# Gated linear attention feeding a cosine-gated layer: x's round trip through memory put ahead of the powers' row in SyncE's queue, and one VectorE pair swapped

## The chip, the core and the metric

The kernel runs on one core of one Trainium2 chip. The metric is the device time of one execution in microseconds (us); lower is better. The core's engines run side by side and wait for each other through semaphores: TensorE (PE, its weight loads shown apart as PEld), VectorE (DVE), ScalarE (ACT), GpSimd (POOL) and SyncE (SP). SP computes nothing here. It issues DMA transfers, one after another in a fixed order, and an issue that has to wait holds up all issues behind it.

## What is computed

The reference, cut to what matters:

```python
# q, k, v, a_re, a_im: (4, 8, 768, 48)
mag = sqrt(a_re**2 + a_im**2); scale = minimum(mag, 0.999) / (mag + 1e-6)
a_re_n, a_im_n = a_re * scale, a_im * scale
for t in range(S):                     # S_re, S_im: 48 x 48 per batch and head
    new_re = ar * S_re - ai * S_im
    new_im = ar * S_im + ai * S_re
    S_re, S_im = new_re + outer(k[t], v[t]), new_im
    y[t] = q[t] @ S_re
x = y.transpose(0, 2, 1, 3).reshape(3072, 384)
h = x @ w_in                           # 384 x 2048
out = (h * cos(h)) @ w_out             # 2048 x 384
```

The first part is a linear recurrence with a complex decay for each step and channel; the second is a two-layer network with the gate h cos h.

## The kernel before

The 768 steps of a batch are cut into chunks of 128, and two chunks make a group: 24 chunks, groups 0 to 11. Inside a chunk the recurrence is done by matmuls: the decays become running sums of logs and angles, keys and queries are scaled and turned by them (tiles ks and qs), keys meet queries in the scores (sc), masked scores (atm) times values plus queries times the running state give y, and the state is moved on to the next chunk with the decay over the whole chunk. That decay is the last row of the powers' tile P. It lies along one partition and is wanted along 96, so it goes out to memory and comes back: `row_out` (L843) writes tile `row`, `row_back` (L848) reads it twice into `end`. `p_end` (L858) then scales `end` on VectorE, after keys and queries were turned.

In the same way y, which is made transposed (tile yT, copied out of PSUM by ScalarE in `f_out`), goes to memory and back to become xT, the layout that the first layer's matmuls read: `f_x` (L1063) issues two writes (x<-yT), `f_xt` (L1072) one read (xT<-x). Matmuls of the first layer are called hp, those of the second op and sum (seven half-size products in place of eight, from group 2 on).

The instructions for groups 0 and 1, and for part of group 2, are written out by hand. From there on a loop (L1721) makes one round for each n from 2 to 11. I call it round n. In round n the kernel works on the scores, state and outputs of group n (`chunks`, L1410), on the logs, powers, keys and queries of group n+1 (`logs`, `prods`, `phases`, `keys`), and on the layers of groups n-1 and n. `weave` (L1363) sets the order: every list of steps gets an interval between 0 and 1, its steps are spread evenly over it, and all are sorted by place. The list `chunks(n)` has the interval 0 to 0.36 and 10 steps (9 in rounds 10 and 11, which load nothing): for each of two chunks two halves of scores, the state and the output; then x and xT (`f_x` and `f_xt`); then the load of keys, queries and values of group n+2. The powers (`prods`) stand from 0.2701 to 0.2735, the first hp matmuls at 0.56. A scheduler then settles the order of instructions on each engine from this order and from what each must wait for; `behind(a, b)` forces a after b on one engine.

Before the change `row_out` and `row_back` were issued at the end of `even_steps` (L822), right after P is done, so at about 0.273; x and xT stood at 0.306. All of these, and the loads of re, im, k, q and v, and the moves that turn keys and queries (tr to memory, then kT and qT back), stand in SyncE's one queue. The load of k can be issued only when VectorE has read the old keys (instruction pair<-k, in `p_apply`, L865), the row only when P is done (lg<-pair,lg; P lives in tile lg), xT only when both writes of x have landed.

In `log_steps` (L736), from group 2 on (PEG = 2), logs are split into a high half (hi, on ScalarE) and a low half (lo, on VectorE), and the product mag*sq, which is the first step of a refined reciprocal, is forced behind lo. The lines L680, L691 and L711 are helpers' lines at which the profile books nearly all ordered instructions of VectorE and ScalarE, TensorE, and ScalarE's table functions.

Of the kernel before, what the change touches and what calls it, by code (L numbers as in the profile page):

```python
# [487 lines left out]
def fast_path(ctx, tc, q, k, v, a_re, a_im, moe_w_in, moe_w_out, out, least, odd, wide,  # L488
# [7 lines left out]
    nc = tc.nc  # L496
    B, H, S, D = q.shape
    DM, DF = moe_w_in.shape
    C = 128
    NCH = S // C  # L500
    G = 2
    N = B * NCH
    NG = N // G
# [30 lines left out]
    late = {}  # L534
    tail = {}

    def chain(ins, engine="scalar"):

        if engine in tail:
            behind(ins, tail[engine])  # L540
        tail[engine] = ins

    def behind(ins, other):
        tc.add_manual_dep(ins.ins, other.ins.name, mybir.DependencyInfo(
            mybir.DependencyClass.NoSync, mybir.DependencyReason.DATA))
# [14 lines left out]
    X = [dict() for _ in range(NG)]  # L560
# [4 lines left out]
    PEG, PER = 2, 1  # L565
# [143 lines left out]
    def special(func, **kw):  # L709
        preload(tables[func])  # L710
        chain(nc.scalar.activation(func=func, **kw))  # L711
# [4 lines left out]
    def temp(tag, bufs=1):  # L716
        return gt.tile([C, G * DM], F32, tag=tag, name=tag, bufs=bufs)
# [5 lines left out]
    def cut(t, i, n):  # L723
        return (flat(t) if len(t.shape) == 4 else t)[:, ds(i * DM, n * DM)]

    def upper_half(g, x, scale):


        for name, tag in ("hi", "rs"), ("lo", "lo"):
            X[g][name] = gt.tile([C, G * DM], F32R, tag=tag, name=name)  # L730
        hi, lo = X[g]["hi"], X[g]["lo"]
        chain(nc.scalar.activation(out=hi, in_=x, func=AF.Copy, scale=scale))
        return lambda: vector.scalar_tensor_tensor(
            out=lo, in0=x, scalar=scale, in1=hi.bitcast(F32), op0=ALU.mult, op1=ALU.subtract)

    def log_steps(g, i, n):  # L736


        x = X[g]
        re, im = cut(x["re"], i, n), cut(x["im"], i, n)  # L740
        if i == 0:
            if g == 0:
                x["sin"] = temp("tan", 2)
            for name in "lg", "tan", "rs":
                x[name] = temp(name, 2 if name == "tan" else 1)
            both = gt.tile([C, 2, G * DM], F32, tag="pair", name="pair")
            x["Q"], x["mag"] = both[:, 0], both[:, 1]
        m2, sq, rs, mag = (cut(x[name], i, n) for name in ("lg", "tan", "rs", "mag"))
        for out_, in_ in (m2, re), (sq, im):
            if g == 0 and i > 0:  # L750
                if in_ is im:
                    yield
                vector.tensor_tensor(out=out_, in0=in_, in1=in_, op=ALU.mult)
            else:
                chain(nc.scalar.activation(out=out_, in_=in_, func=AF.Square))
        vector.tensor_tensor(out=m2, in0=m2, in1=sq, op=ALU.add)
        yield
        special(out=m2, in_=m2, func=AF.Ln, bias=tiny_b)
        special(out=mag, in_=m2, func=AF.Exp, scale=0.5)
        if g == 1:  # L760
            yield
        special(out=rs, in_=m2, func=AF.Exp, scale=-0.5)
        yield
        vector.scalar_tensor_tensor(out=mag, in0=re, scalar=0.0, in1=mag,
                                    op0=ALU.max, op1=ALU.add)
        vector.tensor_scalar(out=m2, in0=m2, scalar1=0.5, scalar2=math.log(CAP),
                             op0=ALU.mult, op1=ALU.min)
        yield
        special(out=rs, in_=rs, func=AF.Ln, scale=EPS, bias=one_b)
        special(out=sq, in_=mag, func=AF.Ln)  # L770
        special(out=sq, in_=sq, func=AF.Exp, scale=-1.0)
        yield
        vector.tensor_tensor(out=m2, in0=m2, in1=rs, op=ALU.subtract)
        yield

        lower = upper_half(g, m2, 1.0) if g >= PEG else None
        if lower:
            X[g]["low"] = lower()
        product = vector.tensor_tensor(out=mag, in0=mag, in1=sq, op=ALU.mult)
        if lower:  # L780
            behind(product, X[g]["low"])
        yield
        vector.scalar_tensor_tensor(out=sq, in0=mag, scalar=2.0, in1=sq,
                                    op0=ALU.subtract, op1=ALU.mult)
        yield
        vector.scalar_tensor_tensor(out=sq, in0=sq, scalar=-1.0, in1=im,
                                    op0=ALU.mult, op1=ALU.mult)
        yield
        junk = stage["pool"].tile([C, DM], BF16, tag="below", name="below", bufs=1) if n == 1 else re
        checked = scalar.activation(out=junk, in_=re, func=AF.Relu, scale=-1.0,  # L790
                                    accum_out=odd[:, ds(next(odds), 1)])
        if g > PEG:
            behind(checked, tail["scalar"])

    def g_log(g, i, n):
        for _ in X[g].pop("steps", None) or log_steps(g, i, n):
            pass
# [24 lines left out]
    def even_steps(g, i, n):  # L822


        x = X[g]
        u = cut(x["mag"], i, n)
        P, Q = cut(x["P"], i, n), cut(x["Q"], i, n)
        ins = [vector.scalar_tensor_tensor(out=u, in0=Q, scalar=HUGE, in1=P,
                                           op0=ALU.min, op1=ALU.mult)]
        yield  # L830
        for t in P, Q:
            ins.append(vector.scalar_tensor_tensor(out=t, in0=u, scalar=3.0, in1=t,
                                                   op0=ALU.subtract, op1=ALU.mult))
            yield

        for one_, what in zip(ins, ("carried", "split")):
            if what in x and g > PEG:
                behind(one_, x[what])
        if g > 0:
            row_out(g, i, n, nc.sync)  # L840
            row_back(g, i, n, nc.sync)

    def row_out(g, i, n, queue):  # L843
        P = cut(X[g]["P"], i, n)
        queue.dma_start(out=X[g]["row"][ds(i * DM, n * DM)],
                        in_=P[C - 1:C].rearrange("o x -> (o x)"))

    def row_back(g, i, n, queue):  # L848
        row = X[g]["row"][ds(i * DM, n * DM)]
        end = X[g]["end"][:, ds(i * H, n * H)]  # L850
        for a in range(2):
            queue.dma_start(out=end[ds(a * D, D)], in_=row.rearrange("(x d) -> d x", d=D))
# [122 lines left out]
    def f_scores(n, hh):  # L975
        y, (g, i) = Y[n], divmod(n, G)
        if i == 0 and hh == 0:
            X[g]["atm"] = ft.tile([C, G, H, C], F32, tag="atm", name="atm", bufs=1)
        y["atm"] = X[g]["atm"][:, i]
        ps = pa.tile([C, HH, C], F32, tag="a", name="sc")  # L980
        for h in range(HH):
            head = hh * HH + h
            matmul(ps[:, h], lhsT=X[n // G]["kT"][:, n % G * H + head],
                   rhs=queries(n, head), start=True, stop=True)
        y["masked"] = vector.tensor_tensor(
            out=y["atm"][:, ts(hh, HH)], in0=ps, in1=causal.unsqueeze(1).to_broadcast([C, HH, C]), op=ALU.mult)
        if "whole" in X[n // G - 1]:
            behind(y["masked"], X[n // G - 1]["whole"])
# [68 lines left out]
    def f_state(n):  # L1057
        if n % NCH < NCH - 1:
            state_sums(n)
            for _ in state_next(n):  # L1060
                pass

    def f_x(g, i=0, n=G):  # L1063

        if i == 0:
            X[g]["moved"] = rows_d.tile([HH, 2, D, G, C], F32, tag="x", name="x")
        for side in range(2):
            late["x"] = nc.sync.dma_start(
                out=X[g]["moved"][:, side, :, ds(i, n)].rearrange("p d g t -> d p g t"),
                in_=X[g]["yT"][ds(side * 64, D), :, ds(i, n)])  # L1070

    def f_xt(g, i=0, n=G):  # L1072

        if i == 0:
            X[g]["xT"] = msb.tile([C, ND, G, C], F32, tag="xT", name="xT")
        moved = X[g]["moved"].rearrange("p s d g t -> (p s d) g t").rearrange("(c r) g t -> r c g t", r=C)
        put = nc.sync.dma_start(out=X[g]["xT"][:, :, ds(i, n)], in_=moved[:, :, ds(i, n)])
        behind(put, late["x"])
        late["x"] = put
# [330 lines left out]
    def chunks(g):  # L1410
        for n in range(g * G, g * G + G):
            for hh in range(2):
                yield lambda n=n, hh=hh: f_scores(n, hh)
            yield lambda n=n: f_state(n)
            yield lambda n=n: f_out(n)
        yield lambda: (f_x(g), f_xt(g))
        if g + 2 < NG:
            yield lambda: load(g + 2, ("k", "q", "v"))

# [423 lines left out]
```

## Time and profile before

| what | value |
|---|---|
| median of 3 runs (lowest to highest) | 659.08 us (659.04 to 659.52) |
| profiled execution, its own time | 662.06 us |
| span of the core in the profiled execution | 660.3 us |
| PE busy | 632.5 us (96%) |
| PEld busy | 573.7 us (87%) |
| DVE busy | 522.4 us (79%) |
| ACT busy | 446.5 us (68%) |
| POOL busy | 30.8 us (5%) |
| SyncE's DMA queue (q1) | 225320 packets, 68.51 MB, 44.9% of 16 engines |
| mean granted TensorE clock | 0.992 of full speed |

TensorE is busy nearly all the time, so what can be won without taking work away lies in its few gaps and in stretches at a lower clock. The profile gives for each group of instructions the idle time of the engine just before them and what ended it. Where several semaphores were waited for, it names the one that came last by its own records. A transfer's issue (SPq rows) is short; its landing comes later and shows in the rows of those that wait, and in the chain of waits.

### The profile page before, as it was taken

The numbers are of one execution on the slowest core, as the hardware profiler recorded it, in microseconds if no ns is written. First come the engines' busy times: TensorE is split into PE (matmuls) and PEld (weight loads), VectorE is DVE, ScalarE is ACT, GpSimd is POOL, SyncE is SP. The second block draws the span as 40 slices with busy tenths as digits, with TensorE's granted clock in tenths as the row PEclk, the third lists the DMA queues.
The fourth block names the chain that finished last, engine by engine and source line by source line (L and its number), as shares of the span: only waits on it lengthen the run. The fifth ranks groups of instructions, "written<-read, shape, count | busy, mean of one in ns | idle before, by whom it ended". The sixth has DMA issues, their size and how long they took to land.

```text
span 660.3 us, 11335 instructions
## 1 busy us (share of the span) xinstructions
PE 632.5 (96%) x4279; PEld 573.7 (87%) x4279; DVE 522.4 (79%) x846; ACT 446.5 (68%) x803; POOL 30.8 (5%) x53
## 2 busy tenths in 40 slices
PE   8999989997999999999999999999999999999996
PEld 5888867675899899899899899899899899999996
DVE  6999979769588799879778868979868969965261
ACT  7898677274597498589489489579579479552340
POOL 4010200000000000000000000000000000000000
PEclk9999989998999999999999999999999999999998
DMA  9977744716716925935935945945855853451001
GB/s 241 243 187 192 229 154 98 179 42 143 210 49 141 282 58 121 253 97 127 252 80 136 252 85 137 244 93 144 229 107 144 229 106 110 129 124 50 24 1 32
DMA packets 232924, 94.95 MB, mean 144 GB/s; under 512 B 208701, under 2 KB 221246, under 8 KB 232858
## 3 DMA queue, kind: packets, MB, share of 16 engines
q1 hardware_dynamic: 225320, 68.51, 44.9%
q0 software_dynamic: 5824, 25.50, 11.8%
q8 instruction: 36, 0.59, 0.4%
q10 hardware_dynamic: 1714, 0.11, 0.2%
q14 instruction: 30, 0.25, 0.1%
HBM read 69.28 MB, written 24.81 MB: 143 GB/s over the span
## 4 chain that ended last, share of the span: by engine, by line
PE 60%; ACT 19%; DVE 8%; DMA 7%; issue 4%; SPq 1%; ACTq 0%; DVEq 0%
PE hp L691 29%; PE op L691 10%; PE sum L691 6%; PE sc L691 4%; DMA xT<-x 3%; PE yp L691 3%; PE hb L691 2%; ACT tan L711 2%; PE sp L691 2%; DMA x<-yT 2%; ACT raw L680 2%; ACT rs L711 2%; ACT L707 2%; ACT yT L680 2%; ACT pair L711 2%
## 5 line engine op out<-in xcount | busy, mean ns | idle before, releaser
L691 PE MATMUL hp<-xT,w_in 128*128 128x256 f32 (+1 forms) x768 | 168.4, 378 | 13.1 <-DMA xT<-x 8.6
L691 PEld LDWEIGHTS hp<-xT,w_in 128*128 128x128 f32 x768 | 143.1, 192 | 35.9 <-DVE qs L680 5.9
L711 ACT ACTIVATE gate<-hp,half_pi_b 128x512 f32<-128x512 f32 x96 | 65.9, 687 | 81.3 <-PE hp L691 65.2
L691 PE MATMUL op<-w_out,gate 128*128 128x192 f32 (+1 forms) x464 | 103.2, 372 | 0.0
L691 PEld LDWEIGHTS op<-w_out,gate 128*128 128x128 f32 x464 | 78.7, 190 | 16.7 <-issue 1.9
L680 DVE TENSOR_TENSOR gate<-hp,gate 128x512 f32<-128x512 f32 x62 | 42.6, 687 | 39.1 <-ACT junk L680 39.0
L680 ACT ACTIVATE junk<-hp 128x512 bf16<-128x512 f32 x96 | 56.6, 590 | 0.0
L691 PE MATMUL sum<-w_out,gate 128*128 128x192 f32 x304 | 54.8, 328 | 0.4 <-DVE gate L680 0.4
L691 PEld LDWEIGHTS sum<-w_out,gate 128*128 128x128 f32 x304 | 49.3, 190 | 0.8 <-DVE gate L680 0.7
L691 PE MATMUL sc<-qT,kT 96*128 96x128 f32 x384 | 49.2, 276 | 0.6 <-issue 0.3
L691 PEld LDWEIGHTS sc<-qT,kT 96*128 96x128 f32 x384 | 46.9, 192 | 2.5 <-issue 1.1
L680 DVE SCALAR_TENSOR_TENSOR gate<-hp,gate 128x512 f32<-128x512 f32 x34 | 23.5, 690 | 22.8 <-ACT junk L680 22.8
L691 PE MATMUL hp<-xh,wh 128*128 128x256 f32 x204 | 36.9, 290 | 0.0
L680 DVE TENSOR_TENSOR atm<-sc,causal 128x512 f32<-128x512 f32 x48 | 32.2, 683 | 5.7 <-PE sc L691 5.7
L691 PE MATMUL hp<-xl,wl 128*128 128x256 f32 x204 | 35.2, 281 | 0.0
L680 ACT COPY yT<-yp 48x512 f32<-48x512 f32 x44 | 25.4, 577 | 14.0 <-PE yp L691 13.3
L691 PE MATMUL yp<-atm,v 128*48 128x128 f32 x352 | 33.6, 277 | 1.1 <-DVE atm L680 1.1
L680 DVE TENSOR_TENSOR gate<-gate 128x256 f32<-128x256 f32 x80 | 31.9, 419 | 3.2 <-PE op L691 2.5
L680 ACT ACTIVATE ot<-sum 128x192 f32<-128x192 f32 x39 | 12.6, 322 | 31.2 <-PE sum L691 31.2
L707 ACT ACT_TABLE_LOAD x24 | 30.8, 1283 | 1.2 <-PEq L1827 0.7
L691 PE MATMUL sum<-t_s,gate 128*128 128x192 f32 x160 | 29.8, 332 | 1.4 <-DVE gate L680 1.2
L691 PEld LDWEIGHTS hp<-xh,wh 128*128 128x128 f32 x204 | 29.7, 189 | 0.5
(163 smaller groups left out, 1246.5 us busy)
## 6 DMA issues: line engine op xcount, KB each, us to landing
moved<-tr SPq DMA_DIRECT2D x20, 768.0 KB
raw<-in_moe_w_in_dram POOLq DMA_DIRECT2D x16, 768.0 KB, 5.6
raw<-in_moe_w_out_dram POOLq DMA_DIRECT2D x16, 768.0 KB, 4.9
kT<-moved SPq DMA_DIRECT2D x40, 192.0 KB
qT<-moved SPq DMA_DIRECT2D x10, 768.0 KB
k<-in_k_dram SPq DMA_DIRECT2D x24, 192.0 KB
q<-in_q_dram SPq DMA_DIRECT2D x24, 192.0 KB
v<-in_v_dram SPq DMA_DIRECT2D x24, 192.0 KB
```

Source lines behind the costliest of these rows:

```text
L680: ins = getattr(self.engine, op)(**kw)
L691: chain(nc.tensor.matmul(out, **kw), "tensor")
L707: chain(nc.scalar.preload_act_table_set(table))
L711: chain(nc.scalar.activation(func=func, **kw))
```

## The change

Three edits belong together. `even_steps` issues the row and its way back only up to group 2; from the fourth group (group 3) on, they are issued by a step of their own, `ends`, in the list `chunks`, behind x and xT and ahead of the loads. `row_out` is there forced behind the last xT. And since `chunks(n)` now has 11 steps for n from 2 to 9 (10 in round 10), each of its steps moves to an earlier place between 0 and 0.36. Apart from that, group 2's product is put ahead of its low half on VectorE, and not forced any more.

```diff
         lower = upper_half(g, m2, 1.0) if g >= PEG else None
-        if lower:
-            X[g]["low"] = lower()
+        if lower and g > PEG:
+            low = lower()
         product = vector.tensor_tensor(out=mag, in0=mag, in1=sq, op=ALU.mult)
-        if lower:
-            behind(product, X[g]["low"])
+        if lower and g > PEG:
+            behind(product, low)
+        elif lower:
+            lower()
...
-        if g > 0:
-            row_out(g, i, n, nc.sync)
-            row_back(g, i, n, nc.sync)
+        if 0 < g <= PEG:
+            ends(g, i, n)
+
+    def ends(g, i=0, n=G):
+        row_out(g, i, n, nc.sync)
+        row_back(g, i, n, nc.sync)
...
-        queue.dma_start(out=X[g]["row"][ds(i * DM, n * DM)],
-                        in_=P[C - 1:C].rearrange("o x -> (o x)"))
+        put = queue.dma_start(out=X[g]["row"][ds(i * DM, n * DM)],
+                              in_=P[C - 1:C].rearrange("o x -> (o x)"))
+        if g > PEG:
+            behind(put, late["x"])
...
         yield lambda: (f_x(g), f_xt(g))
+        if PEG < g + 1 < NG:
+            yield lambda: ends(g + 1)
         if g + 2 < NG:
             yield lambda: load(g + 2, ("k", "q", "v"))
```

SyncE's queue in round 2, before, from the last output of group 1's first half to the loads for group 4:

```order
L1253 DMA out_dram<-ot 128x384
L845 DMA row<-lg 1x768
L1068 DMA x<-yT 48x4x256 x2
L852 DMA end<-row 48x16x1 x2
L584 DMA k<-in_k_dram 128x8x48
L1077 DMA xT<-x 128x3x256
L584 DMA k<-in_k_dram 128x8x48
L584 DMA q<-in_q_dram 128x8x48 x2
L584 DMA v<-in_v_dram 128x8x48 x2
```

The same stretch of the changed kernel (its lines are shifted by 5 to 9):

```order
L1260 DMA out_dram<-ot 128x384
L1075 DMA x<-yT 48x4x256 x2
L584 DMA k<-in_k_dram 128x8x48 x2
L1084 DMA xT<-x 128x3x256
L850 DMA row<-lg 1x768
L584 DMA q<-in_q_dram 128x8x48 x2
L859 DMA end<-row 48x16x1 x2
L584 DMA v<-in_v_dram 128x8x48 x2
```

x is now first, the row comes after xT, and both loads of k stand between x and xT where one stood before. Rounds 3 to 9 read the same way; round 10 has x, xT, row, end and no loads.

VectorE in round 2, before, where the masks (atm) of the second chunk's scores stand among the logs of group 3:

```order
L680 TENSOR_TENSOR lg<-lg,rs 128x768
L680 SCALAR_TENSOR_TENSOR lo<-lg,hi 128x768
L680 TENSOR_TENSOR pair<-pair,tan 128x768
L680 TENSOR_TENSOR atm<-sc,causal 128x512
L680 SCALAR_TENSOR_TENSOR tan<-pair,tan 128x768
L680 TENSOR_TENSOR atm<-sc,causal 128x512
L680 SCALAR_TENSOR_TENSOR tan<-tan,im 128x768
```

And in the changed kernel:

```order
L680 TENSOR_TENSOR lg<-lg,rs 128x768
L680 TENSOR_TENSOR atm<-sc,causal 128x512
L680 SCALAR_TENSOR_TENSOR lo<-lg,hi 128x768
L680 TENSOR_TENSOR pair<-pair,tan 128x768
L680 TENSOR_TENSOR atm<-sc,causal 128x512
L680 SCALAR_TENSOR_TENSOR tan<-pair,tan 128x768
L680 SCALAR_TENSOR_TENSOR tan<-tan,im 128x768
```

The first mask moved ahead of lo and pair, the second ahead of tan; on TensorE the score halves that they mask moved ahead of four or eight op matmuls likewise.

ScalarE in round 10, before, around the powers of group 11 (lg and pair from the sums lgs), with the copies of the second chunk's outputs (yT):

```order
L680 ACTIVATE raw<-raw 128x768
L711 ACTIVATE lg<-lgs 128x384
L680 ACTIVATE raw,odd<-raw,least_e_b 128x768
L711 ACTIVATE pair<-lgs 128x384
L711 ACTIVATE lg<-lgs 128x384
L711 ACTIVATE pair<-lgs 128x384
L707 ACT_TABLE_LOAD
L711 ACTIVATE tan<-tan 128x768
L680 COPY yT<-yp 48x4x128 x2
```

And in the changed kernel:

```order
L680 ACTIVATE raw<-raw 128x768
L680 ACTIVATE raw,odd<-raw,least_e_b 128x768
L680 COPY yT<-yp 48x4x128 x2
L711 ACTIVATE lg<-lgs 128x384
L711 ACTIVATE pair<-lgs 128x384
L711 ACTIVATE lg<-lgs 128x384
L711 ACTIVATE pair<-lgs 128x384
L707 ACT_TABLE_LOAD
L711 ACTIVATE tan<-tan 128x768
```

In this round alone the output copies moved ahead of the powers, as on TensorE the second chunk's output matmuls (yp) moved ahead of the sums lgs.

## Prediction

> **What bounds the kernel now.** I read the page first: PE is busy 632.5 us of a span of 660.3 us, so I went to what TensorE waits for. The longest row of its waits is this (total us, times, longest):
>
> ```profile
> PE hp L691 <- DMA xT<-x: 8.6, 6, 3.4
> ```
>
> Next I took TensorE's timeline at the first hp matmuls of rounds 2 to 9. In brackets stands the idle time before them and what ended it:
>
> ```profile
> 162.16 13.14 PE L691 MATMUL hp<-xT,w_in 128*128 128x256 f32 x53 [3.44 <-DMA xT<-x]
> ...
> 216.07 4.15 PE L691 MATMUL hp<-xT,w_in 128*128 128x256 f32 x18 [1.47 <-DMA xT<-x]
> ...
> 268.59 6.71 PE L691 MATMUL hp<-xT,w_in 128*128 128x256 f32 x30 [0.65 <-DMA xT<-x]
> ...
> 318.61 10.60 PE L691 MATMUL hp<-xT,w_in 128*128 128x256 f32 x48 [1.20 <-DMA xT<-x]
> ...
> 369.39 10.60 PE L691 MATMUL hp<-xT,w_in 128*128 128x256 f32 x48 [1.20 <-DVE ks L680]
> ...
> 420.15 10.60 PE L691 MATMUL hp<-xT,w_in 128*128 128x256 f32 x48 [0.92 <-DMA xT<-x]
> 469.96 10.38 PE L691 MATMUL hp<-xT,w_in 128*128 128x256 f32 x47 [0.96 <-DVE qs L680]
> ...
> 520.40 10.60 PE L691 MATMUL hp<-xT,w_in 128*128 128x256 f32 x48 [0.86 <-DMA xT<-x]
> ```
>
> Every round from 2 to 9 stops once, 10.70 us in all. I count the two that name VectorE with the others, since hp reads nothing of ks or qs, and xT leaves as late in them. Around round 2's stop the granted clock dropped. The columns are the stretch, its length, PE's busy time with the count of hp matmuls, the granted clock, DMA share, GB/s:
>
> ```profile
> 158.27:161.68 3.41, 0.00 (x0) 1.00 0.91 203
> 161.68:165.10 3.42, 2.94 (x7) 0.50 1.11 223
> ```
>
> After a stretch nearly without work TensorE ran at half speed for 3.42 us, so its 2.94 busy us held what takes 1.47 at full speed.
>
> **Part 1, the queue: two kinds of rounds.** Round 2 on SyncE, then the end of xT's flight in the chain of waits, then VectorE:
>
> ```profile
> 149.08 0.36 SPq L1253 DMA_DIRECT2D out_dram<-ot  x1
> 154.78 0.24 SPq L845 DMA_DIRECT2D row<-lg  x1
> 155.08 0.80 SPq L1068 DMA_DIRECT2D x<-yT  x2
> ...
> 157.35 0.54 SPq L584 DMA_DIRECT2D k<-in_k_dram  x1
> 158.35 0.38 SPq L1077 DMA_DIRECT2D xT<-x  x1
> ```
>
> ```profile
> 158.35 3.76 DMA xT<-x
> ```
>
> ```profile
> 152.03 0.95 DVE L680 TENSOR_TENSOR pair<-k,pair 128x768 f32<-128x768 f32 x1
> ...
> 153.77 0.95 DVE L680 SCALAR_TENSOR_TENSOR lg<-pair,lg 128x768 f32<-128x768 f32 x1
> ```
>
> x waits behind the row, the row for P at 154.72. Without it x can go at 149.5, behind the output. But both loads of k now stand ahead of xT, and they wait for pair<-k. So xT's new time hangs on when VectorE reads the keys. Here that is 152.98, 1.74 before P. How soon k follows, and how long a pair's issue takes, shows where nothing else held it, in the hand-written part:
>
> ```profile
> 104.92 0.95 DVE L680 TENSOR_TENSOR pair<-k,pair 128x768 f32<-128x768 f32 x1
> ```
>
> ```profile
> 105.89 1.02 SPq L584 DMA_DIRECT2D k<-in_k_dram  x2
> ```
>
> At once (105.87 to 105.89), and 1.02 us for both. So round 2's xT is issued at about 154.2 instead of 158.35, and lands 3.76 later, at 158.0, or 158.8 if one load of k more stands in its way (a load is 192 KB; the row below of loads alone gives 231 GB/s, so 0.85 us). TensorE was ready at 162.16 - 3.44 = 158.72. I take the whole 3.44 as won, and the half clock with it: 1.47.
>
> ```profile
> DMA packets 3664, 0.69 MB, mean 231 GB/s; under 512 B 3664, under 2 KB 3664, under 8 KB 3664
> ```
>
> How small a rest of the stop would bring the half clock back? The stop of 2.43 us before 88.63 (quoted below) did:
>
> ```profile
> 90.00:93.42 3.42, 3.42 (x10) 2.89 (x9) 3.38 (x5) 0.00 (x0) 0.00 (x0) 0.50 0.58 110
> ```
>
> [...]
>
> Rounds 5 and 8 are of the same kind, because as in round 2 the group after them starts a batch and has no carry to wait for. Round 5, VectorE then SyncE:
>
> ```profile
> 308.31 0.95 DVE L680 TENSOR_TENSOR pair<-k,pair 128x768 f32<-128x768 f32 x1
> ```
>
> ```profile
> 314.56 0.38 SPq L1077 DMA_DIRECT2D xT<-x  x1
> ```
>
> Keys are read at 309.26, 5.3 us before xT's issue, so both loads can be out 4 us before it, and x, freed from the row, goes ahead of them. An issue 1.2 us earlier is all that is needed. Both stops go: 1.20 + 0.96 = 2.16.
>
> Rounds 3, 4, 6, 7 and 9 are of the other kind. Round 7, SyncE then VectorE:
>
> ```profile
> 412.50 0.24 SPq L845 DMA_DIRECT2D row<-lg  x1
> ...
> 415.14 0.47 SPq L584 DMA_DIRECT2D k<-in_k_dram  x1
> 416.30 0.45 SPq L1077 DMA_DIRECT2D xT<-x  x1
> 416.80 1.05 SPq L584 DMA_DIRECT2D k<-in_k_dram  x1
> ```
>
> ```profile
> 413.49 0.95 DVE L680 TENSOR_TENSOR pair<-k,pair 128x768 f32<-128x768 f32 x1
> ```
>
> Keys are read only at 414.44. The loads take SyncE until 415.5, so xT goes at 415.5 to 416.1 (the second load took 1.05 in this row) instead of 416.30: 0.2 to 0.8 earlier. Against that stands one load of 0.85 us more in front of it. For it speaks that the way back of the row, which lay in front of xT before, now lies behind. From below, the whole stop goes (all five: 1.47 + 0.65 + 1.20 + 0.92 + 0.86 = 5.10); from above, each xT lands up to 0.85 - 0.2 = 0.65 later, 3.3 us lost. I take 0.2 a round, 1.0, the row nearest to it being round 7's.
>
> [...]
>
> **Part 2, chunks' earlier places.** In round 2 TensorE stopped twice for masks:
>
> ```profile
> 143.90 0.42 PE L691 MATMUL yp<-atm,v 128*48 128x128 f32 x4 [0.72 <-DVE atm L680]
> ...
> 145.36 0.43 PE L691 MATMUL yp<-atm,v 128*48 128x128 f32 x4 [0.38 <-DVE atm L680]
> ```
>
> Both masks now stand one or two VectorE steps of 0.95 us ahead, and their score halves before op matmuls, so I take both stops as won, 1.1 (bounds 0 and 1.1); what follows in the round, pair<-k too, moves up with them. Against it: hp then starts some 4.5 us earlier, while VectorE turns keys and queries as before, and only after that frees hp's first buffer. I put 0.5 for a stop there (0 to 1.0).
>
> Round 10 has no stop to win, but there the powers of group 11 now wait for the outputs. VectorE's first product of hp follows its transposes without a pause:
>
> ```profile
> 573.86 2.29 DVE L680 STREAM_TRANSPOSE tr<-qs 128x1536 f32<-128x1536 f32 x1
> 576.04 0.67 DVE L680 TENSOR_TENSOR gate<-hp,gate 128x512 f32<-128x512 f32 x1
> ```
>
> and the outputs take TensorE 1.9 us (first and last row of the eight):
>
> ```profile
> 555.11 0.43 PE L691 MATMUL yp<-atm,v 128*48 128x128 f32 x4
> ...
> 556.68 0.39 PE L691 MATMUL yp<-qT,state 96*48 96x128 f32 x4
> ```
>
> That delay runs through powers, keys and their move to the scores of round 11. I charge 1.0 of it (0 to 1.9).
>
> **Part 3, the product.** VectorE waited 1.33 us for ScalarE's high half with the product queued behind:
>
> ```profile
> 87.75 0.96 DVE L680 SCALAR_TENSOR_TENSOR lo<-lg,hi 128x768 fp32r<-128x768 f32 x1 [1.33 <-ACT hi L732]
> 88.63 4.12 PE L691 MATMUL hp<-xT,w_in 128*128 128x256 f32 x12 [2.43 <-ACT raw L680]
> ```
>
> The product fills that wait, lo stays where it was, and VectorE is 0.87 us ahead. TensorE's stop beside it is ended by neither, and it has no other until 143.90. I take 0; at most 0.87 won, and nothing lost, since lo cannot come later than its wait.
>
> **The sum.** Won: 3.44 + 1.47 + 2.16 + 1.0 + 1.1 = 9.17. Lost: 0.5 + 1.0. Together 7.7 us. The profiled execution has 662.06 us (span 660.3 and 1.8 around it), which becomes 654.4. The median is 3.0 lower, 659.08, and becomes 651.4.
>
> **Rivals.** *A: the row's way back was the brake.* Its small pieces lay in front of xT, and with them gone the five rounds lose their whole stop: 5.10 in place of 1.0, so 647.3. For it speaks that x, xT and the row's return left within 4 us of each other in round 7; against it, that two loads take their place. Chance 0.15.
>
> *B: the next wait takes it back.* Scores need kT and qT, moved by the same queue from VectorE's transposes, which no xT makes earlier. In round 4 the scores started the moment after such a wait could end:
>
> ```profile
> 236.45 1.13 PE L691 MATMUL sc<-qT,kT 96*128 96x128 f32 x8 [0.31 <-issue]
> ```
>
> If half of what is won at hp is lost there, 4 us stay: 655. Chance 0.15. If nearly all, nothing stays: 659; the round's period is then VectorE's, not TensorE's, which its 79% speaks against. Chance 0.08.
>
> *C, slower: end comes too late.* `end` now follows x, two k, xT, row and two q. In round 7, from xT at 416.1 with 0.45 and 0.24 for xT and row and 1.05 for each q, its issue falls near 419 and, with a flight like xT's 3.76, its landing near 423. VectorE wants it after its transposes, and hp's products queue behind it:
>
> ```profile
> 423.33 2.22 DVE L680 STREAM_TRANSPOSE tr<-qs 128x1536 f32<-128x1536 f32 x1
> ```
>
> That is 425.55, 2.5 later; and hp's three buffers last until 428.1 (three quarters of 10.60 from 420.15), about 1.1 longer than the first product needs. So it decides once `end` lands over 3.6 us later than worked out. At 5 us late it costs 1.4 in each of 8 rounds, 11.2 - 7.7 = 3.5 in all: 662.6. Against it: 3.6 is as much as a whole flight. Chance 0.07.
>
> **How the numbers follow.** Forecast 0.55, A 0.15, B 0.15 and 0.08, C 0.07. A measurement of this kernel can tell 0.2%, 1.3 us, from no change. Faster: 0.55 + 0.15 + 0.15 = 0.85; same 0.08; slower 0.07. The range takes in the unknown costs: at best 5.1 us under the forecast (five whole stops, no cost in round 10), 646.3; at worst the five rounds lose 3.3 (4.3 worse) and round 10 costs 0.9 more, 656.6. I give 646.5 to 657.
>
> **What would show it.** Right: x issued before the row in every round, hp's stop in rounds 2, 5 and 8 gone, no half clock near 160, stops of about 0.5 to 1.3 left in the five others with xT issued right behind the second k. Wrong: those five stops gone too (A), new stops at sc after hp (B), VectorE waiting at `end` (C), or a stop at hp in round 2 although xT left by 154.5.

## The result, and the profile after

The changed kernel takes 650.31 us (median of 7 runs, 649.74 to 655.16) against 659.04 for the kernel before (median of 7 runs beside it): a ratio of 0.9891 with a 95% interval of 0.9859 to 0.9922, so 5.1 to 9.3 us are won. The forecast was 651.4 us, between 646.5 and 657.0. The profiled execution took 651.08 us, 10.98 less than the one of before.

Again TensorE's waits come first (total us, times, longest):

```profile
PE hp L691 <- DMA xT<-x: 5.2, 5, 1.8
PE sum L691 <- DVE gate L680: 2.0, 5, 0.5
PE sc L691 <- issue: 1.8, 1, 1.8
...
PE hp L691 <- DVE gate L680: 0.7, 1, 0.7
```

The wait for xT has come down from 10.70 us in eight rounds to 5.2 in five. One wait is new, that of hp for a product of VectorE, and the one at the scores (sc) has grown from 0.31 to 1.81 us. TensorE's timeline at the first hp of rounds 2 to 9:

```profile
152.70 2.54 PE L691 MATMUL hp<-xT,w_in 128*128 128x256 f32 x11
...
206.59 3.72 PE L691 MATMUL hp<-xT,w_in 128*128 128x256 f32 x16 [1.84 <-DMA xT<-x]
...
260.52 1.75 PE L691 MATMUL hp<-xT,w_in 128*128 128x256 f32 x7 [0.54 <-DMA xT<-x]
309.20 2.10 PE L691 MATMUL hp<-xT,w_in 128*128 128x256 f32 x9
...
359.84 1.53 PE L691 MATMUL hp<-xT,w_in 128*128 128x256 f32 x6 [1.34 <-DMA xT<-x]
410.44 1.75 PE L691 MATMUL hp<-xT,w_in 128*128 128x256 f32 x7 [0.31 <-DMA xT<-x]
459.11 2.10 PE L691 MATMUL hp<-xT,w_in 128*128 128x256 f32 x9
...
509.56 1.75 PE L691 MATMUL hp<-xT,w_in 128*128 128x256 f32 x7 [1.16 <-DMA xT<-x]
```

Rounds 2, 5 and 8 have no stop left. The other five stop for 5.19 us in all, where they had stopped for 5.10. SyncE's queue in round 2 shows why rounds like it are free:

```profile
145.80 0.90 SPq L1075 DMA_DIRECT2D x<-yT  x2
147.18 1.17 SPq L584 DMA_DIRECT2D k<-in_k_dram  x2
149.23 0.37 SPq L1084 DMA_DIRECT2D xT<-x  x1
149.70 0.28 SPq L850 DMA_DIRECT2D row<-lg  x1
```

x goes first, 3.09 us before P is done at 148.89. VectorE has read the old keys at 147.15, and the loads of k follow at once. They are out while xT still waits for x to land, and xT goes 3.43 us after x, before the row. The stretches around the start of hp hold no half clock any more (columns: the stretch, its length, busy time with the count of instructions of PE, PEld, DVE, ACT and POOL, the granted clock, DMA share, GB/s):

```profile
149.29:152.70 3.41, 3.41 (x14) 2.29 (x13) 2.36 (x5) 2.24 (x4) 0.00 (x0) 1.00 1.02 244
152.70:156.12 3.42, 3.42 (x17) 3.03 (x17) 3.30 (x5) 2.14 (x5) 0.00 (x0) 1.00 1.07 163
```

Not all of the 10.98 us is the change's. The stop of 2.43 us at 88.63, and the half clock behind it (3.42 us of work at half speed, 1.71 lost), are missing in the profile after: 4.14 us that, as the first experiment shows, come and go with either order of VectorE's pair.

### The profile page after: what moved, and what is told of

It reads as the page before. It is cut to its first block, busy times and chain, and to the rows that moved or that the text cites. A ratio compares the mean times of both kernels' runs of the same rounds, so it can differ in the third digit from the quotient of the medians.

```text
span 649.3 us, 11364 instructions
## 1 busy us (share of the span) xinstructions
PE 629.3 (97%) x4279; PEld 571.5 (88%) x4279; DVE 522.2 (80%) x846; ACT 446.4 (69%) x803; POOL 30.8 (5%) x53
## 4 chain that ended last, share of the span: by engine, by line
PE 69%; ACT 10%; DVE 8%; DMA 7%; issue 3%; SPq 1%; ACTq 0%; DVEq 0%
PE hp L691 29%; PE op L691 13%; PE sum L691 8%; PE sc L691 5%; PE yp L691 4%; DMA xT<-x 4%; PE sp L691 3%; PE hb L691 3%; DMA im<-in_a_im_dram 2%; DVE pair L680 2%; ACT tan L711 1%; DVE tan L680 1%; ACT rs L711 1%; PE phs L691 1%; SPq L584 1%
## 5 line engine op out<-in xcount | busy, mean ns | idle before, releaser
L691 PE MATMUL hp<-xT,w_in 128*128 128x256 f32 (+1 forms) x768 | 165.6, 373 | 5.9 <-DMA xT<-x 5.2
L691 PEld LDWEIGHTS hp<-xT,w_in 128*128 128x128 f32 x768 | 141.5, 190 | 27.2 <-DVE qs L680 4.4
L691 PE MATMUL sc<-qT,kT 96*128 96x128 f32 x384 | 51.0, 278 | 2.1 <-issue 1.8
```

The costliest lines, as they stand in the source:

```text
L691: chain(nc.tensor.matmul(out, **kw), "tensor")
```

## The experiments

From the fourth one on, VectorE and ScalarE were held, instruction by instruction, to the order that they have in the changed kernel (a list of their instructions, each forced behind the one ahead of it), and TensorE's matmuls keep theirs too, so that SyncE's or GpSimd's part alone differs; line numbers are shifted by it. Ratios are to the kernel before, run on the same chip. The stops, in us, are read from TensorE's timeline of each profile; a dash is under 0.1. The column hp has the stop at the first hp of rounds 2 to 9, the last column that at the scores of round 4.

| kernel | median us, ratio (95%) | hp, rounds 2 to 9 | sc |
|---|---|---|---|
| before | 659.04 | 3.44 1.47 0.65 1.20 1.20 0.92 0.96 0.86 | 0.31 |
| changed | 650.31, 0.9891 (0.9859 to 0.9922) | - 1.84 0.54 - 1.34 0.31 - 1.16 | 1.81 |
| swap alone | 658.31, 0.9997 (0.9965 to 1.0029) | 3.39 1.68 0.82 1.16 1.34 1.05 1.16 0.70 | 0.48 |
| queue alone | 652.62, 0.9890 (0.9851 to 0.9929) | - 1.75 0.86 - 0.86 1.59 - 0.78 | 1.82 |
| places alone | 657.76, 0.9973 (0.9950 to 0.9995) | 3.45 1.54 0.34 1.08 1.48 0.20 1.27 0.83 | 0.57 |
| loads behind xT, 8 rounds | 647.98, 0.9832 (0.9790 to 0.9874) | none | 1.94 |
| loads behind xT, 5 rounds | 646.93, 0.9791 (0.9762 to 0.9820) | none | 2.50 |
| weight load later | 648.79, 0.9828 (0.9796 to 0.9860) | - 2.01 - - 0.87 - - 0.86 | - |
| both of these | 646.08, 0.9783 (0.9753 to 0.9814) | none | - |
| row in front, 5 rounds | 650.06, 0.9833 (0.9800 to 0.9867) | - 0.26 - - - - - - | 2.34 |
| row in front, 8 rounds | 648.44, 0.9840 (0.9785 to 0.9896) | 1.83 - - - 0.13 - - - | 1.39 |
| row and x in front | 657.64, 0.9971 (0.9944 to 0.9999) | 2.98 1.30 0.41 0.52 1.78 - 0.55 - | 2.83 |

**The swap alone.** To the kernel before:

```diff
-        if lower:
-            X[g]["low"] = lower()
+        if lower and g > PEG:
+            low = lower()
         product = vector.tensor_tensor(out=mag, in0=mag, in1=sq, op=ALU.mult)
-        if lower:
-            behind(product, X[g]["low"])
+        if lower and g > PEG:
+            behind(product, low)
+        elif lower:
+            lower()
```

> The kernel before with part 3 alone (group 2's product ahead of its low half on VectorE). My theory: nothing, a ratio of 1.000 (within 0.2%), because TensorE does not wait for either of the two; a stop of some 2.4 us before the hp matmuls near 88 us, where the profile has one, comes from a late xT and has nothing to do with the swap. Rival: the swap is what took that stop and the half clock behind it out of the changed kernel's profile; then this kernel is 3.5 to 4 us faster, a ratio near 0.994, and no stop stands near 88 us.

The median does not move. (Beside the swap, the scheduler moved one row and one load of im in the hand-written part of SyncE's queue.) In its profile the stop at 88 us is missing, as the rival had it; but it is missing in the kernel with the earlier places alone too, which has the old product, and it stands in "row in front, 5 rounds", which has the new one. There, TensorE's timeline:

```profile
88.15 2.83 PE L778 MATMUL hp<-xT,w_in 128*128 128x256 f32 x12 [1.69 <-DMA xT<-x]
```

So the stop comes and goes with either product. In this kernel the profile names xT as what ended it; before the change it had named a tile of ScalarE (raw). Why it comes in one profile and not in another, no run shows. What the swap does win shows without that stop: in both kernels with the old product and no early stop TensorE waits for VectorE's low half of the angles. Places alone:

```profile
97.78 0.45 PE L691 MATMUL phs<-lo,exact 128*128 128x384 f32 x1 [0.55 <-DVE lo L680]
```

With the swap this row has no wait: 0.55 us, too little for the medians.

**The queue alone.** The changed kernel with the old product, and `ends` called in the step of x, so that `chunks` keeps 10 steps:

```diff
-        yield lambda: (f_x(g), f_xt(g))
-        if PEG < g + 1 < NG:
-            yield lambda: ends(g + 1)
+        yield lambda: (f_x(g), f_xt(g), PEG < g + 1 < NG and ends(g + 1))
```

> The changed queue alone: x, both k, xT, row, end in SyncE's queue, the list chunks kept at 10 steps and the product as before, so that TensorE and ScalarE keep their order of before. My theory: the queue carries the gain. hp's stops of rounds 2, 5 and 8 go (3.44 + 1.20 + 0.96) with round 2's half clock (1.47), the other five stay near their 5.1 in all, the two mask stops of round 2 (1.1) stay: about 6.5 to 7 us faster, 652 to 652.5, a ratio near 0.990. Rival (the earlier places of the chunks' steps did it): under 2 us faster, a ratio above 0.997, and round 2's stop stays above 2 us.

**The earlier places alone.** The kernel before with a step that does nothing:

```diff
         yield lambda: (f_x(g), f_xt(g))
+        if PEG < g + 1 < NG:
+            yield lambda: None
```

> The kernel before with an empty eleventh step in the list chunks of rounds 2 to 10, so that scores, state, outputs and x get the changed kernel's earlier places, with SyncE's queue of rounds 2 to 9 as before. My theory: only the mask stops of round 2 go (0.72 + 0.38) and hp still waits for xT in all eight rounds: 0.5 to 1.5 us faster, a ratio of 0.998 to 0.999. Rival (earlier places carry the gain): 5 us or more, a ratio under 0.993, with the stops of rounds 2, 5 and 8 gone.

(In the queue alone VectorE also takes cut<-xT ahead of `end` in seven rounds, two short instructions that the scheduler exchanged.) Both came out as my theory had it: the queue carries the gain (652.62 against 659.35 on the same chip, 6.7 us), the places the masks' 1.10 (657.76, so 1.6; by the interval 0.3 to 3.3). Yet places alone holds a surprise. Its stop of 3.45 us in round 2 has no half clock behind it. The stop, the two stretches over which it lies, and the one behind them (columns as above):

```profile
157.13 3.07 PE L691 MATMUL hp<-xT,w_in 128*128 128x256 f32 x13 [3.45 <-DMA xT<-x]
```

```profile
152.26:155.67 3.41, 1.42 (x5) 0.54 (x3) 2.43 (x3) 2.77 (x4) 0.00 (x0) 1.00 0.83 124
155.67:159.09 3.42, 1.96 (x9) 1.75 (x10) 3.42 (x4) 0.00 (x0) 0.00 (x0) 1.00 1.17 264
159.09:162.50 3.41, 3.41 (x18) 3.00 (x17) 2.92 (x4) 1.26 (x3) 0.00 (x0) 1.00 1.13 341
```

In the queue alone, a stop of only 1.82 us has one behind it:

```profile
227.32:230.74 3.42, 1.60 (x14) 1.43 (x13) 2.82 (x4) 3.19 (x7) 0.00 (x0) 1.00 0.44 110
230.74:234.15 3.41, 3.41 (x15) 3.41 (x14) 2.71 (x5) 3.39 (x7) 0.00 (x0) 0.50 0.00 0
```

The last section comes back to this.

**Loads behind xT, in all 8 rounds.** The changed kernel with the loads of `chunks`, the outputs and the moved keys behind xT:

```diff
-            yield lambda: load(g + 2, ("k", "q", "v"))
+            yield lambda: load(g + 2, ("k", "q", "v"), put=lambda **kw: behind_x(nc.sync.dma_start(**kw)))
...
+    def behind_x(put):
+        behind(put, late["x"])
```

> The changed kernel with both loads of k (and all of q, v, the outputs and the moved keys) held behind xT in SyncE's queue in rounds 2 to 9; VectorE, ScalarE and TensorE keep the changed kernel's order, instruction by instruction. My theory: in rounds 3, 4, 6, 7 and 9 what holds xT is the wait of the k loads for the instruction that reads the old keys, so with them behind it xT goes right after x has landed, some 2 us earlier, and the five stops (5.2 us in all) go: 645 to 646, a ratio near 0.980 against the kernel before. Rival B: the wait for qT and kT at the scores takes it back: stops at sc of 1 us and more in several rounds, and 649 to 651. Rival: the later k loads or row are wanted in time by VectorE: VectorE waits at pair<-k or at end, and the kernel is slower than the changed one.

All stops of hp for xT go, but the time, 647.98 us, lies between my 645 to 646 and rival B's 649 to 651: the scores now stop in round 9 as well, which rival B had:

```profile
477.90 1.13 PE L778 MATMUL sc<-qT,kT 96*128 96x128 f32 x8 [1.57 <-DMA qT<-moved]
```

Its stop of 1.94 us at the scores of round 4 also has a half clock behind it: 3.41 us from 227.75, all of them busy at a granted clock of 0.50, so 1.71 us lost. The changed kernel's stop of 1.81 us there has none (1.00 from 228.41). Three of the kernels below, loads behind xT in 5 rounds, row in front in 5 rounds, and row and x in front, had a mean granted clock of 0.996 in the profiled execution, the changed kernel 0.999; in the first of them eight matmuls of the scores took 1.93 us right behind this stop, where they took 1.06 in weight load later.

**The same in rounds 3, 4, 6, 7 and 9 alone; the weight load of round 3 later; and both.** The first has `behind_x` only where n % 3 != 2 for round n; the second is one line of `guarded`:

```diff
-            yield lambda: wait_for(X[g]["gate"][NJ // 2 - 1][0:1, 0, 0:1])
+            yield lambda: wait_for(X[g]["gate"][X[g]["order"][-1]][0:1, 0, 0:1])
```

> The changed kernel with k, q, v and the moved keys held behind xT in rounds 3, 4, 6, 7 and 9 alone; rounds 2, 5 and 8, which have no stop at hp, keep the changed queue. All engines but SyncE keep their order. My theory: the five stops at hp (5.2 us) go as they did with the loads held back in all eight rounds, and the stop of 1.57 us that came up there at the scores of round 9 does not, because it came from round 8's loads: 0.5 to 1.5 us faster than with all eight, 646 to 647, a ratio of 0.979 to 0.982. Rival: that stop comes from elsewhere and stays.

> The changed kernel with one word changed: GpSimd's weight load in round 3 waits for the last gate of the round, as the others do, and not for the second, so it starts some 15 us later. All engines keep their order. In the changed kernel this load moves beside kT and qT of round 3, and the scores of round 4 stop for 1.81 us. My theory: the load's big packets hold up the many small ones of kT; with it gone from there qT lands 12 to 13.5 us after the transposes and not 16.8, the stop at the scores of round 4 goes, and no half clock follows: 1.5 to 2 us faster than the changed kernel, near 648.5, a ratio of 0.985 to 0.987. Rival: qT is late because the queue's loads of k, q and v, which the change moved, are still under way; then the stop stays at 1.5 us or more.

> Both edits on top of the changed kernel: GpSimd's weight load of round 3 later, and the loads behind xT in rounds 3, 4, 6, 7 and 9. If the two costs are independent, the gains add: 5 us and 1.8 us less than the changed kernel, 643.5 to 645, a ratio of 0.976 to 0.979, with no stop over 1 us left at hp or at the scores. Rival: the scores' wait for qT takes part of it in other rounds: 646 to 647.

With the five rounds alone the stop of round 9 is gone, so it came from holding the loads back in rounds 2, 5 and 8, most likely in round 8, right before it. SyncE in round 7 of the changed kernel, and then of this one:

```profile
399.42 2.16 SPq L1075 DMA_DIRECT2D x<-yT  x2
405.01 1.02 SPq L584 DMA_DIRECT2D k<-in_k_dram  x2
406.14 0.67 SPq L1084 DMA_DIRECT2D xT<-x  x1
```

```profile
400.09 0.81 SPq L1166 DMA_DIRECT2D x<-yT  x2
403.31 0.39 SPq L1175 DMA_DIRECT2D xT<-x  x1
403.80 0.28 SPq L937 DMA_DIRECT2D row<-lg  x1
404.37 1.02 SPq L1519 DMA_DIRECT2D k<-in_k_dram  x2
```

In the changed kernel k stands at the head of the queue until the old keys are read, and xT goes 6.72 us after x; freed from it, xT goes after 3.22 us, as soon as x has landed.

The scores of round 4 wait for qT of round 3. Beside its move GpSimd loads a block of weights in the changed kernel, and with the one line changed only some 17 us later:

```profile
216.25 0.74 POOL L631 DMA_DIRECT2D raw<-in_moe_w_in_dram  x1 [0.58 <-ACT junk L680]
```

```profile
233.77 0.74 POOL L717 DMA_DIRECT2D raw<-in_moe_w_in_dram  x1 [0.32 <-issue]
```

Seven microseconds of DMA from 1.3 us after the first kT issue, changed kernel and then weight load later (packets, MB, share of the 16 engines):

```profile
q1 hardware_dynamic: 6071, 0.78, 70.8%
q0 software_dynamic: 208, 0.79, 35.1%
```

```profile
q1 hardware_dynamic: 6479, 1.36, 96.6%
```

208 packets of weights took a third of the engines, and SyncE's queue moved 0.78 MB in place of 1.36. Without them the stop at the scores goes, with the loads of k, q and v where they were, so these alone do not make it. Before the change this block was loaded beside the move too, but 2.15 us behind the first kT in place of 0.56, and the stop was 0.31. Not all of the delay is the block's: in the changed kernel the first kT went 5.57 us after the moves to memory were issued, in place of 4.17, before the block was loaded at all, and no run shows why. And 1.17 of its 1.81 us come back a little later in round 4, which I had not expected: a wait for VectorE's gates, 0.5 in the changed kernel, is 1.67 here. By the times this kernel is not quite clear of the changed one, since their intervals meet at 0.986.

```profile
245.75 1.57 PE L778 MATMUL sum<-t_s,gate 128*128 128x192 f32 x8 [1.67 <-DVE gate L766]
```

So both edits together give 646.08 and not the 643.5 to 645 that I expected. By the median it is the fastest version here. Its interval (0.9753 to 0.9814) lies under the changed kernel's, but overlaps that of the loads behind xT in 5 rounds (0.9762 to 0.9820).

**The row in front of xT.** Three queues that put parts of the old order back: x, row, end, xT, k in five rounds; the same in all eight; and row, x, end, xT, k in all eight, where k alone has left its old place. The core of the first two:

```diff
-        yield lambda: (f_x(g), f_xt(g))
-        if PEG < g + 1 < NG:
-            yield lambda: ends(g + 1)
+        yield lambda: f_x(g)
+        yield lambda: (ends(g + 1), f_xt(g))
```

and in the third the steps are `ends(g + 1)` and then `(f_x(g), f_xt(g))`, with x behind the row. In all three the loads are behind xT.

> The changed kernel with the queue x, row, end, xT, k, q, v in rounds 3, 4, 6, 7 and 9: the row's way back stands ahead of xT again, and the loads of k behind it. It prices rival A, the row as the brake of these rounds. If the row were the brake and the loads of k none, the five stops stay as they are, 5 us in all or more (650 to 651). If the loads of k alone hold xT, the stops go as without the row (646 to 647). I expect something near the first: P is done only about 1 us before the keys are read, so the row holds xT nearly as long: 3 to 5 us of stops left, 649 to 651, a ratio of 0.985 to 0.988.

> The changed kernel with the queue x, row, end, xT, k, q, v in all rounds from 2 to 9: x is ahead of the row, but the row's way back stays in front of xT as it was before the change. In rounds 3, 4, 6, 7 and 9 this cost no stop over 0.3 us. In rounds 2, 5 and 8 the powers are done 1.7 us after the keys are read, so xT has to wait longer: P, then 1.2 to 2.6 us of the row's flight, then 0.9 for the two issues of end. My theory (there the row's way back is a brake of its own): a stop of 1 to 3 us at hp in round 2 and up to 1 us in rounds 5 and 8; 651 to 653 in all, a ratio of 0.986 to 0.990. Rival (only x's place mattered): no stop over 0.3 us in any of the eight rounds, 647 to 649.

> The changed kernel with the queue row, x, end, xT, k, q, v in rounds 2 to 9: of the queue before the change only the loads of k are moved, behind xT; x stays behind the row. My theory: before the change it was x behind the row, and with it the powers, that held xT, not k, so taking k away brings nothing: about 3 us of stop in round 2, 0.5 to 1.5 us in each of the others, 655 to 658, a ratio of 0.994 to 0.998. Rival (k ahead of xT was a brake before the change too): the stops of rounds 3, 4, 6, 7 and 9 go, 650 to 653.

The first missed what I expected: I had 3 to 5 us of stops, it has 0.26 at hp in these rounds. Its median, 650.06, is within what I expected, but not for that reason: its profile has the early stop quoted above and 2.34 at the scores, and a mean granted clock of 0.996. In the second, round 2 stops for 1.83 (and round 6 for 0.13), and rounds 5 and 8 do not; its time, 648.44, is the rival's and not my 651 to 653. The third has most of it back: 7.54 us of stops where there were 10.70, and all but about 2 us of the time. TensorE's waits, row in front in 8 rounds, and row and x in front:

```profile
PE hp L778 <- DMA xT<-x: 1.8, 1, 1.8
```

```profile
PE hp L778 <- DMA xT<-x: 7.5, 6, 3.0
```

So before the change what held xT was, in the main, x behind the row, hence behind the powers. What k alone added there is small: the five rounds stop for 3.49 us without it, and for 5.10, 5.59 and 4.39 with it, in the kernel before and in the two with its queue (swap alone, places alone). And with x ahead of the row, the row's way back mattered in round 2 alone.

## Why the prediction was right, point by point

The terms, against the pair of profiled executions (won is positive):

| step | forecast | measured |
|---|---|---|
| round 2's stop | 3.44 | 3.44 |
| the half clock behind it | 1.47 | 1.47 |
| rounds 5 and 8 | 2.16 | 2.16 |
| rounds 3, 4, 6, 7, 9 | 1.0 | -0.09 (5.10 to 5.19) |
| masks of round 2 | 1.1 | 1.10 |
| hp's next buffer in round 2 | -0.5 | -0.67 |
| powers of round 10 | -1.0 | 0 |
| the product | 0 | 0 here, 0.55 without the early stop |
| scores of round 4 | not in the sum | -1.50 (0.31 to 1.81) |
| sums waiting for gates | not in the sum | -0.3 (1.7 to 2.0) |

That makes 5.6 us; the early stop and its half clock make another 4.14, and 1.2 of the 10.98 are in smaller pieces. By the medians 8.7 were won, by the ratio 7.2, where I had 7.7. The terms of my own sum come to 7.4, because the misses of the five rounds and of round 10 nearly cancel. The scores and sums that I had left out cost 1.8 more, and how much of the early stop is in the medians no run shows. So it is in part luck that the total came so near.

**Right:** the mechanism of rounds 2, 5 and 8. Queue alone shows that the queue does it, and row and x in front shows which part: x's place ahead of the row. In round 2 xT's place ahead of the row counts as well, by the 1.83 of row in front in 8 rounds. The half clock went too, but places alone shows that such a stop does not always bring one, so 1.47 is what this pair of executions won.

**Mis-sized: the five rounds.** I took 0.2 us a round from an issue 0.2 to 0.8 earlier and up to 0.85 of a load in front. Both came, and cancelled. In round 7 VectorE reads the old keys until 404.98, and xT is issued 1.16 later where it had been 1.86:

```profile
404.03 0.95 DVE L680 TENSOR_TENSOR pair<-k,pair 128x768 f32<-128x768 f32 x1
```

And xT's flights in the chain of waits, rounds 3 and 7 before, then the same after, are 0.31 and 0.44 longer:

```profile
212.34 3.69 DMA xT<-x
...
416.30 3.72 DMA xT<-x
```

```profile
202.56 4.00 DMA xT<-x
...
406.14 4.16 DMA xT<-x
```

The brake was only exchanged: x used to wait behind the row for the powers, and now xT waits behind k for the reading of the keys, which on VectorE come close together. That one load more in front of xT costs it 0.85 us was my estimate, from 192 KB at 231 GB/s. The flights grew by 0.31 and 0.44, about half of that at most, and whether the load is what lengthened them no run shows. In the five rounds nothing was won (5.10 to 5.19).

**Wrong: round 10.** I charged 1.0 for powers that wait for the outputs. They do, but the sums of angles (phs), which come next on the way to keys and queries, have a fixed place in TensorE's order, and that place comes 10.61 us earlier, as the start of that round's hp does (10.60: 569.85 to 559.25). Before, then after:

```profile
563.47 0.47 PE L691 MATMUL phs<-hi,exact 128*128 128x384 f32 x1
```

```profile
552.86 0.47 PE L691 MATMUL phs<-hi,exact 128*128 128x384 f32 x1
```

I followed the delay along VectorE and ScalarE and overlooked that both wait for TensorE there.

**Rivals.** A, the row's way back as the brake of the five rounds, did not come, and with x ahead of it the row costs 0.26 at most there. B came in one place, at 1.50 us: the wait for qT in round 4. So one of the signs that I had named for being wrong, a new stop at sc, did show. Its cause was not that TensorE came earlier against the transposes, as B had it: it was ready for the scores 15.14 us after their end, where it had been 14.96. What came later was qT, beside the weight load, which I had not seen. C did not come: after the transposes of round 7 VectorE takes `end` without a pause.

```profile
416.00 0.52 DVE L680 TENSOR_SCALAR cut<-xT 128x768 uint32<-128x768 uint32 x1
416.43 0.16 DVE L680 TENSOR_SCALAR end<-end 96x16 f32<-96x16 f32 x1
```

## What to carry to other kernels

When a transfer is taken out from in front of another in a queue, read what now stands there and what that waits for: here the same five stops stayed, with another name. The transfer that TensorE waits for goes right behind its own data, and loads that wait for an engine go behind it, unless they can go while it still waits for its data, as in rounds 2, 5 and 8. And a delay on one engine is to be followed only as far as the next thing that waits for another engine anyway.

## What the runs showed of the hardware

Within the kernels the half clock comes in stretches of 3.41 us, and in the profile of before its starts lie whole multiples of 3.413 us apart (90.00 and 161.68, 21 of them; 161.68 and, at the kernel's end, 656.62, 145 of them). It stood behind stretches of 3.41 us in which TensorE was idle for 1.82 us (queue alone, from 227.32), 1.94 (loads behind xT in 8 rounds, from 224.34), 2.04 and 2.96 (before, from 86.59 and 158.27). Behind 1.46 and 1.99 (places alone, from 155.67 and 152.26) and behind 1.74 and 1.84 (changed, from 225.00 and 204.52) there was none. The length of the stop orders these less well: 1.82 us were enough in queue alone, and the 3.45 of places alone, which fell on two stretches, 1.99 and 1.46, were not. Why 1.82 and 1.94 had one behind them and 1.84 and 1.99 did not, no run shows. No run of its own tried this; it is read from traces made for other ends.
